# Second matmul of a PReLU feed-forward in 32-row tiles: three groups in lanes, the fourth tile fills

## The chip, the cores and the metric

The kernel runs on one core of one Trainium2 chip. The metric is the device time of one execution in microseconds (us), as the median of several runs. Engines are called as in the profile: PE is TensorE's matmuls, PEld its weight loads, DVE is VectorE, ACT is ScalarE, POOL is GpSimd, SP is SyncE, which issues DMAs here.

## The reference

Two steps follow each other: an induced set attention over four batches of 12480 tokens with 128 channels and 32 inducing points, then a feed-forward with a leaky activation and 2048 hidden features, applied to all 49920 tokens.

```
def mab(q, kv):
    a = softmax(q @ kv.T / sqrt(128))
    return a @ kv
h   = mab(inducing, x[b])      # 32 x 128, one per batch
y   = mab(x[b], h)             # 12480 x 128
z   = y @ w_in                 # 49920 x 2048
g   = max(z, 0) + alpha * min(z, 0)
out = g @ w_out                # 49920 x 128, float32
```

## The kernel before

Tokens are handled in groups of 512 (GRP), four groups to a block of 2048; a batch has six blocks and a rest of 192 tokens, so 25 groups, and there are 100 groups in all. The 2048 hidden features are 16 chunks of 128.

The attention's second step and the first matmul of the feed-forward are folded: hW = h @ w_in has only 32 rows per chunk, so the first matmul ("fill") takes the 32 rows of hW of a chunk as weights and streams the 512 unnormalized attention weights (rep) of a group. It uses 32 of TensorE's 128 rows; the four row tiles can hold four different chunks. rep holds the same 32 rows four times, once for each row tile. The activation is split as g = alpha * z + (1 - alpha) * max(z, 0): the first part is linear and goes through one small matrix per batch (hA = h @ Amat, 32 x 128), the second needs max(z, 0) alone, with (1 - alpha) scaled into w_out (W1). The softmax denominator (rd) is multiplied in at the end.

So the steps for a group are: 16 fills into PSUM banks; 16 evictions with max(., 0) to bf16 tiles gt in SBUF, on ACT (line 448) or DVE (line 450); the second matmul (mm2), in which a 128x128 block of gt (tokens) is the stationary operand and the 128x128 chunk of W1 streams, 64 matmuls per group, summed in an accumulator bank of 128x512 float32; the linear part (linear), 4 matmuls of 32 rows into the same accumulator; and the output (finish, line 503), a multiplication by rd on DVE into ob, which a DMA on POOL's queue writes out.

The work goes in slots. A slot makes four fills, one in each row tile (fill), then runs the tasks due there, then the 16 second matmuls of the slot before (mm2). A group has four slots (two for the rest of 192). PSUM's eight banks are a ring of six, given out in turn by bank(), and two accumulators, used alternately. A planner (make_plan), a beam search with fixed costs and due times, picks for each slot which of the four evictions go to ACT and where an output stands among them. Every instruction of an engine is chained to the one before it (pin), so the order on each engine is the order in which the code emits it.

Tasks are the attention's remaining steps, spread over slots by the table tasks: loading and transposing the next batch's tokens (a_load, a_xpose), its scores and sums (a_scores, a_accum), h (h_sum, h_den, h_transpose), hW and hA (h_weights, h_linear), and for each block the scores of tokens against h (b_scores), their replication by way of DRAM (b_rep) and the denominators (b_den). The first batch's h is made ahead of the first slot, on TensorE. All matmuls go through the helper mm, line 96; the tiles tell them apart in the profile.

Of the kernel before, what the change touches and what calls it, by code (L numbers as in the profile page):

```python
# [16 lines left out]
P = 128  # L17
# [4 lines left out]
RING = 6  # L22
# [3 lines left out]
def kernel(  # L26
# [47 lines left out]
    xn_pool = ctx.enter_context(tc.tile_pool(name="xnp", bufs=8))  # L74
    xt_pool = ctx.enter_context(tc.tile_pool(name="xtp", bufs=2))
    gt_pool = ctx.enter_context(tc.tile_pool(name="gtp", bufs=4))
# [9 lines left out]
    ring = [psum.tile([P, GRP], f32, name=f"ring{i}") for i in range(RING)]  # L86
    accs = [psum.tile([P, NB, C], f32, name=f"acc{i}") for i in range(2)]
    ring_n = [0]

    def bank():  # L90
        t = ring[ring_n[0] % RING]
        ring_n[0] += 1
        return t
# [59 lines left out]
    def p_xpose(st, u, i, last=False):  # L153
        xn = st.xn[u]
        if u == NS:
            tp = bank()[:].bitcast(bf16)
            for j in range(JR):
                pin(nc.tensor.transpose(
                    tp[:, j * PR : (j + 1) * PR], xn[:, j, :], ident[:PR, :PR]
                ))  # L160
            pin(nc.vector.tensor_copy(
                out=st.xTr[:].rearrange("c j p -> c (j p)"), in_=tp[:, :REM]
            ))
            return
        cut = 2 if last else 1
        for h in range(cut):
            tp = bank()[:].bitcast(bf16)
# [9 lines left out]
            if h == 0:  # L177
                pin(nc.vector.tensor_copy(out=dst, in_=tp[:, :w]))  # L178
            else:
                pin(nc.scalar.copy(out=dst, in_=tp[:, :w]))  # L180

# [8 lines left out]
    def p_scores(st, u, i):  # L190
# [9 lines left out]
        ))  # L200
        st.e1T[u, i] = e1t
# [20 lines left out]
    def warm(st, n=1):  # L222
        for _ in range(n):
            mm(
                accs[0][:, 1:, :].rearrange("p k c -> p (k c)"), ident[:],
                st.xT[:, 0, 0, : 3 * P], start=False, stop=False, skip_group_check=True,
            )
# [6 lines left out]
    def p_scale(st, et):  # L234
        ps = bank()
        mm(ps[:, 0:1], fold[:], et[:])
        st.rs = const.tile([P, 1], f32, name="rs")
        st.sc = st.rs
        pin(nc.vector.reciprocal(out=st.rs[:], in_=ps[:, 0:1]))

# [22 lines left out]
    def a_scores(st, u):  # L263
        ps = bank()
        if u < NS:
# [5 lines left out]
            ))  # L271
            e1T = work.tile([P, NB, P], bf16, name="e1T", tag="e1T")
            pin(nc.sync.dma_start_transpose(out=e1T[:], in_=e1[:]))
        else:
# [5 lines left out]
            ))  # L280
            e1T = work.tile([P, JR, M], bf16, name="e1Tr", tag="e1Tr")
# [5 lines left out]
    def a_accum(st, u):  # L287
# [3 lines left out]
        if u < NS:  # L291
# [10 lines left out]
            ))  # L302
        else:
# [7 lines left out]
            ))  # L311

# [5 lines left out]
    def h_den(st):  # L318
# [5 lines left out]
        pin(nc.vector.tensor_scalar_mul(out=st.fr[:], in0=fold[:], scalar1=rh[:]))  # L324


    def h_transpose(st):
# [3 lines left out]
        pin(nc.vector.tensor_copy(out=st.hT4[:], in_=ps[:, :P]))  # L331
        st.hT = st.hT4[:, 0:M]

    def h_weights(st, first=False):
        ps = bank()
        for r in range(4):
            mm(
                ps[32 * r : 32 * r + 32, :], st.hT,
                w_in_b[:, r * NJ * P : (r + 1) * NJ * P],
            )  # L340
        st.hW = work.tile([P, NJ, P], bf16, name="hW", tag="hW")

        for j0, j1 in ((0, 1), (1, NJ)) if first else ((0, NJ),):
            evac_h(
                st, st.hW[:, j0:j1, :].rearrange("m j k -> m (j k)"), ps[:, j0 * P : j1 * P]
            )

    def h_linear(st):
# [3 lines left out]
        evac_h(st, st.hA[:], pa[:, :C])  # L352


    def b_scores(st, s):
# [12 lines left out]

        nq = NQ if s < NS else 1
# [14 lines left out]
    def b_scores_pe(st, q):  # L384
# [6 lines left out]
        ))  # L391
        st.rep[q] = st.rep0[:, q, :]

    def b_den(st, s):
        e2 = st.e2.pop(s)
        ps = bank()
        if s < NS:
            for j in range(NB):
                mm(ps[:, j * NQ : (j + 1) * NQ], e2[:, j * P : (j + 1) * P], pick[:])
            rd = work.tile([P, NB, NQ], f32, name="rd", tag="rd")  # L400
# [3 lines left out]
        else:  # L404
            for j in range(JR):
                mm(ps[:PR, j : j + 1], e2[:, j * PR : (j + 1) * PR], pick[0:M, 0:1])
            rd = work.tile([PR, JR, 1], f32, name="rdr", tag="rdr")
            pin(nc.vector.reciprocal(
                out=rd[:].rearrange("p j q -> p (j q)"), in_=ps[:PR, :JR]
            ))  # L410
        st.rden[s] = rd
# [5 lines left out]

    held = []

    def flush():  # L420
        while held:
            finish(*held.pop())

    def fill(st, g, j):
        pp, nb, cp = shape_of(g)
        t = pp * nb
        w = t * cp
        rep = st.rep[g]
        gt = gt_pool.tile([P, 4, GRP], bf16, name="gt", tag="gt")
        banks = []  # L430
        for r in range(4):
            ps = bank()
            for i in range(cp):
                mm(
                    ps[:, i * t : (i + 1) * t],
                    st.hW[32 * r : 32 * r + 32, j * cp + i, :],
                    rep[32 * r : 32 * r + 32, :t],
                )
            banks.append(ps)
        lin = j == NJ // cp - 1 and lin_groups(st.b, g)  # L440
        if lin:
            linear(st, lin)
        bits, pos = plan[st.b * NG + g, j]
        for r, ps in enumerate(banks):
            if r == pos:
                flush()
            if bits >> r & 1:
                pin(nc.scalar.activation(out=gt[:, r, :w], in_=ps[:, :w], func=RELU))  # L448
            else:
                pin(nc.vector.tensor_relu(gt[:, r, :w], ps[:, :w]))  # L450
        flush()
        return gt

    def mm2(st, g, j, gt):
        pp, nb, cp = shape_of(g)
        acc = accs[(st.b * NG + g) % 2]
        begun = (g % 2 == 1 and st.b + g > 1) or cp > 1
        for r in range(4):
            for i in range(cp):
                c = r * NJ + j * cp + i  # L460
                for k in range(nb):
                    k0 = (i * nb + k) * pp
                    mm(
                        acc[:pp, k, :], gt[:, r, k0 : k0 + pp], W1[:, c, :],
                        start=(j == 0 and r == 0 and i == 0 and k == 0 and not begun),
                        stop=False, skip_group_check=True,
                    )
        if j == NJ // cp - 1 and st.b * NG + g > 0:
            held.append((st, g))

    def lin_groups(b, g):
        if g % 2 == 0 and (b, g) != (0, 0):
            return [g, g + 1] if g + 1 < NS * NQ else [g]
        return []

    def linear(st, groups):
        for k in range(NB):  # L480
            for r, g in enumerate(groups):
                pp, nb, cp = shape_of(g)
                if k < nb:
                    mm(
                        accs[(st.b * NG + g) % 2][:pp, k, :],
                        st.rep[g][32 * r : 32 * r + 32, k * pp : (k + 1) * pp],
                        st.hA[32 * r : 32 * r + 32, :],
                        start=((r == 1 or cp > 1) and k == 0), stop=False, skip_group_check=True,
                    )

    def finish(st, g):
        pp, nb, _ = shape_of(g)
        acc = accs[(st.b * NG + g) % 2]
# [3 lines left out]
        final = (st.b, g) == (B - 1, NG - 1)  # L497
# [8 lines left out]
        if final:  # L506
            pin(nc.scalar.activation(  # L507
                out=ob[:pp, cut, :], in_=acc[:pp, cut, :], func=COPY, scale=rd[:pp, cut, 0:1]
            ))
        t0 = st.b * N + s * SUP  # L510
# [4 lines left out]
        ending = st.b == B - 1 and g >= NG - 4  # L515
        pin((nc.sync if ending else nc.gpsimd).dma_start(out=dst, in_=ob[:pp, :nb, :]))  # L516
        st.rep.pop(g)


# [4 lines left out]
    xs = const.tile([P, NQ, GRP], f32, name="xs")  # L524
# [17 lines left out]
    w_out_f = const.tile([P, KC, C], f32, name="w_out_f")  # L542
    pin(nc.gpsimd.dma_start(out=w_in_b[:], in_=moe_w_in))
    w_out_v = moe_w_out.rearrange("(r j p) c -> p r j c", p=P, j=NJ)
# [19 lines left out]
    itp = bank()[:].bitcast(bf16)  # L564
    nc.tensor.transpose(itp[:, :M], ind_b[:], ident[:M, :M])  # L565
    nc.vector.tensor_copy(out=IT[:], in_=itp[:, :M])

# [10 lines left out]
    def alphas():  # L578
# [5 lines left out]
        ))  # L584

# [15 lines left out]
    def w_amat():  # L601
# [6 lines left out]
        pin(nc.vector.tensor_copy(out=Amat[:], in_=aps[:, :C]))  # L608

# [6 lines left out]
    pool = accs[0][:, 0, :M]  # L616
    den = accs[1][:, 0, 0:1]
# [3 lines left out]
    for i in range(n):  # L621
# [7 lines left out]
        if i == 3:  # L629
# [12 lines left out]
    h_weights(st, first=True)  # L642
# [5 lines left out]
    fills = [(b, g, j) for b in range(B) for g in range(NG)  # L648
             for j in range(NJ // shape_of(g)[2])]
    states = {0: st}  # L650
    tasks = {}


    def at(slot, fn, j=1, cost=None):
        tasks.setdefault((slot, j), []).append((fn, cost))

    def late_finish():
        linear(st, [0])
        finish(st, 0)

    at(0, lambda: warm(st, 2), 0)
    at(0, lambda: b_scores_pe(st, 1), 1, (240, "A", 480))
    at(0, lambda: b_den(st, 0), 2, (130, "D", 250))
    at(1, w_amat, 2, (950, "D", 250))
    at(1, lambda: h_linear(st), 3, (80, "D", 250))
    at(2, late_finish, 0)
    at(2, lambda: linear(st, [1]), 0)

    for b in range(B):
        base = b * NG  # L670
        for s in range(1, NS + 1):
            g = base + s * NQ - 4
            at(g, lambda b=b, s=s: b_scores(states[b], s), 3, (320, "A", 490))
            at(g + 1, lambda b=b, s=s: b_rep(states[b], s), 3)
            at(g + 2, lambda b=b, s=s: b_den(states[b], s), 3, (130, "D", 250))
        if b + 1 < B:
            n = b + 1

            def begin(n=n):
                states[n] = new_batch(n)  # L680

            at(base, begin)
            for i, u in enumerate(order):
# [131 lines left out]
```

## Time and profile before

| | |
|---|---|
| Time, median of 3 runs (lowest, highest) | 592.75 us (592.55, 592.86) |
| Profiled execution: span from first to last instruction | 591.0 us |
| Time outside the span, against the median | 1.75 us |
| PE, PEld, DVE, ACT, POOL busy | 578.7, 434.2, 517.7, 502.5, 84.9 us |
| First fill, end of the last second matmul | 25.5, 587.7 us |
| Granted TensorE clock | 1.000 |
| DMA | 70.10 MB, mean 119 GB/s |

All times are us from the start of the span unless marked ns. A line of a group gives line, engine, operation, output<-input, partitions x elements, and a count; then the busy time, the mean ns of one, the idle time of the engine just before them, and what ended most of that. "32*128" ahead of a matmul's shape says that it uses 32 rows and 128 columns of the array. A matmul's duration reaches from its start to its modelled end; matmuls overlap, so the distance of their starts is what a stream of them costs. In a timeline, a line is start, length, engine, operation and how many were merged into it.

### The profile page before, as it was taken

How to read it: one execution, taken by the hardware profiler on the slowest of the kernel's cores; microseconds unless marked ns; L12 is line 12 of the kernel's file. 1: busy time of each engine (PE TensorE's matmuls, PEld its weight loads, DVE VectorE, ACT ScalarE, POOL GpSimd, SP SyncE). 2: the span in 40 equal slices, each digit the busy share in tenths (PEclk: the TensorE clock that was granted, in tenths of full speed). 3: DMA queues.
4: the chain of work that ended last, by engine and by line, in shares of the span. 5: the costliest groups of instructions: out<-in, count | busy, mean ns of one | idle time of the engine just before them, and what ended most of it. 6: DMA issues, size and time to landing. Idle time of an engine off the chain costs nothing.

```text
span 591.0 us, 21769 instructions
## 1 busy us (share of the span) xinstructions
PE 578.7 (98%) x9218; PEld 434.2 (73%) x9219; DVE 517.7 (88%) x869; ACT 502.5 (85%) x988; POOL 84.9 (14%) x170
## 2 busy tenths in 40 slices
PE   5999999999999999999999999999999999999997
PEld 4677777777777777777777777777777777777776
DVE  3688998999889989998989899988988998998996
ACT  2579888888889988888888998888888988989987
POOL 6631111101011111110111111101101101101100
PEclk9999999999999999999999999999999999999999
DMA  9973978751237569953126597985122221221211
GB/s 198 210 174 90 177 149 163 154 140 55 86 87 165 125 128 185 171 137 92 60 83 142 121 163 129 185 159 131 59 70 80 89 93 54 92 91 56 94 47 62
DMA packets 81825, 70.10 MB, mean 119 GB/s; under 512 B 55440, under 2 KB 71072, under 8 KB 81728
## 3 DMA queue, kind: packets, MB, share of 16 engines
q0 software_dynamic: 12528, 38.51, 26.0%
q1 hardware_dynamic: 69056, 29.68, 25.0%
q8 instruction: 72, 1.18, 0.8%
q10 hardware_dynamic: 144, 0.52, 0.2%
q14 instruction: 25, 0.20, 0.1%
HBM read 40.20 MB, written 28.75 MB: 117 GB/s over the span
## 4 chain that ended last, share of the span: by engine, by line
PE 97%; DVE 1%; DMA 1%; ACT 1%; issue 0%; SPq 0%
PE acc L96 68%; PE ring L96 27%; PE ring L172 1%; DMA ind_f<-in_inducing_dram 1%; ACT gt L448 0%; DVE xT L178 0%; DVE gt L450 0%; DVE ob L503 0%; DVE xn L612 0%; ACT xT L180 0%; SPq L526 0%; ACT ob L507 0%; DVE hT L246 0%; DVE ind_b L562 0%; PE ring L565 0%
## 5 line engine op out<-in xcount | busy, mean ns | idle before, releaser
L448 ACT ACTIVATE gt<-ring 128x512 bf16<-128x512 f32 x899 | 469.5, 599 | 67.8 <-ACT gt L448 27.4
L450 DVE TENSOR_SCALAR gt<-ring 128x512 bf16<-128x512 f32 x669 | 435.1, 685 | 52.2 <-PE ring L96 37.8
L96 PE MATMUL acc<-W,gt 128*128 128x128 bf16 x6272 | 417.9, 220 | 0.2 <-DVE ob L503 0.2
L96 PEld LDWEIGHTS <-gt 128*128 128x128 bf16 x6272 | 352.4, 98 | 79.6 <-issue 76.8
L96 PE MATMUL ring<-rep,hW 32*128 32x512 bf16 (+1 forms) x1600 | 157.3, 379 | 0.0
L516 POOL DMA_DIRECT2D out_dram<-ob x96 | 51.8, 540 | 476.5 <-DVE ob L503 412.6
L96 PEld LDWEIGHTS <-hW 32*128 32x128 bf16 x1600 | 41.1, 91 | 41.6 <-issue 0.5
L503 DVE TENSOR_TENSOR ob<-acc,rd 128x512 f32<-128x512 f32 x96 | 65.4, 681 | 2.5 <-PE acc L96 2.5
L96 PE MATMUL acc<-hA,rep 32*128 32x128 bf16 x392 | 19.8, 214 | 0.0
L96 PEld LDWEIGHTS <-rep 32*128 32x128 bf16 x392 | 15.6, 93 | 5.6
L129 POOL DMA_DIRECT2D xn<-in_x_dram x28 | 15.3, 551 | 3.3 <-DMA xn<-in_x_dram 2.4
L197 ACT ACTIVATE e1t<-ring 128x256 bf16<-128x256 f32 (+1 forms) x13 | 4.8, 371 | 10.5 <-PE ring L96 10.4
L178 DVE COPY xT<-ring 128x1024 bf16<-128x1024 bf16 (+1 forms) x12 | 8.0, 669 | 5.2 <-PE ring L172 4.8
L361 ACT ACTIVATE e<-ring 128x512 bf16<-128x512 f32 x18 | 11.0, 612 | 0.0
L269 ACT ACTIVATE e<-ring 128x512 bf16<-128x512 f32 x18 | 10.9, 605 | 0.0
L96 PE MATMUL ring<-xT,hT 128*32 128x512 bf16 (+1 forms) x97 | 10.0, 389 | 0.0
L172 PE MATMUL ring<-ident,xn 128*128 128x128 bf16 x96 | 8.8, 249 | 0.9 <-DVE xn L612 0.9
L172 PEld LDWEIGHTS <-xn 128*128 128x128 bf16 x96 | 6.8, 112 | 1.0 <-DVE xn L612 1.0
L96 PEld LDWEIGHTS <-hT 128*32 128x32 bf16 (+1 forms) x122 | 3.7, 92 | 5.1 <-issue 2.6
L96 PE MATMUL ring<-xn,e1T 128*32 128x128 bf16 x288 | 7.4, 221 | 0.0
L96 PE MATMUL ring<-xT,IT 128*32 128x512 bf16 x72 | 7.2, 390 | 0.0
L565 PE MATMUL ring<-ident,ind_b 32*128 32x32 bf16 x1 | 0.2, 205 | 6.1 <-DVE ind_b L562 6.1
(87 smaller groups left out, 113.6 us busy)
## 6 DMA issues: line engine op xcount, KB each, us to landing
out_dram<-ob POOLq DMA_DIRECT2D x93, 256.0 KB, 2.9
rep<-e2d SPq DMA_DIRECT2D x92, 128.0 KB, 3.4
xn<-in_x_dram POOLq DMA_DIRECT2D x18, 512.0 KB, 6.7
e2d<-e SPq DMA_DIRECT2D x24, 128.0 KB, 2.0
xn<-in_x_dram POOLq DMA_DIRECT2D x10, 256.0 KB, 8.5
w_out_f<-in_moe_w_out_dram POOLq DMA_DIRECT2D x4, 256.0 KB, 11.1
out_dram<-ob SPq DMA_DIRECT2D x3, 256.0 KB, 2.3
xs<-in_x_dram ACTq DMA_DIRECT2D x1, 512.0 KB, 4.9
```

Of the source, the lines that this page charges most:

```text
L96: return pin(nc.tensor.matmul(o, lhsT, rhs, start=start, stop=stop, **kw))
L129: pin(nc.gpsimd.dma_start(out=xn[:, i * w : (i + 1) * w, :], in_=src[:, i * w : (i + 1) * w, :]))
L172: pin(nc.tensor.transpose(tp[:, k * P : (k + 1) * P], xn[:, q, j * C : (j + 1) * C], ident[:]))
L178: pin(nc.vector.tensor_copy(out=dst, in_=tp[:, :w]))
L197: pin(nc.scalar.activation(out=e1t[:pp, :nb, :].rearrange("p k m -> p (k m)"), in_=ps[:pp, : nb * M], func=EXP, scale=scale,))
L269: pin(nc.scalar.activation(out=e1[:], in_=ps[:], func=EXP, scale=scale, accum_out=st.es[:, u : u + 1]))
L361: pin(nc.scalar.activation(out=e2[:], in_=ps[:], func=EXP, scale=scale_of(st)))
L448: pin(nc.scalar.activation(out=gt[:, r, :w], in_=ps[:, :w], func=RELU))
L450: pin(nc.vector.tensor_relu(gt[:, r, :w], ps[:, :w]))
L503: pin(nc.vector.tensor_tensor(out=ob[:pp, :cut, :], in0=acc[:pp, :cut, :], in1=rbc, op=MULT))
L516: pin((nc.sync if ending else nc.gpsimd).dma_start(out=dst, in_=ob[:pp, :nb, :]))
L565: nc.tensor.transpose(itp[:, :M], ind_b[:], ident[:M, :M])
```

## The change

The second matmul is split by rows for 13 of the 16 chunks (NROW). A chunk's 128x128 matmul becomes four matmuls of 32 rows each, one per row tile. Three groups are worked on at a time, each in a lane; a lane stays in one row tile for a stretch and moves to the next tile for the next, so that after four stretches a group has had all four quarters of its 13 chunks. Lanes start one stretch apart, with one stretch in four without a start. A round of a stretch takes the next chunk of each lane: four steps (k) of up to three pieces, each with its own 32x128 block of gt as weights and 32 rows of W1 streaming, and one fill in the fourth row tile. The first round of a lane in a stretch also has one of the four linear matmuls. A lane's chunk is left out of a round where its eviction is not done yet by the code's own clock, and the fill where no bank is due to be free.

After the stretch stands a drain of TensorE; then come outputs, the other three chunks of the groups as whole 128-row matmuls (whole), and the tasks of that cycle. There are 126 such cycles. The first two groups, the four rests of 192 tokens and two of the last groups do not go in lanes: the first two are done in eight opening slots as before, the others with whole chunks between stretches.

The ring and the two accumulators become one pool of eight banks: bank() takes the idle bank that is free soonest, and drained() returns it, with times from a running clock (clk), which also decides between ACT and DVE for each eviction in place of make_plan. gt tiles hold one chunk, 64 of them instead of 4 of four chunks. hW is kept for all 16 chunks in each of the four row tiles (h_weights: four matmuls and four evictions instead of four small matmuls side by side and one eviction). To make room, xs and w_out_f share a buffer and there are six xn buffers instead of eight.

```diff
+NBANK = 8
+NROW = 13
+AHEAD = 2
+KEPT = 60
...
-    xn_pool = ctx.enter_context(tc.tile_pool(name="xnp", bufs=8))
+    xn_pool = ctx.enter_context(tc.tile_pool(name="xnp", bufs=6))
-    gt_pool = ctx.enter_context(tc.tile_pool(name="gtp", bufs=4))
+    gt_pool = ctx.enter_context(tc.tile_pool(name="gtp", bufs=KEPT + 4))
...
     def bank():
-        t = ring[ring_n[0] % RING]
-        ring_n[0] += 1
-        return t
+        i = min(idle, key=lambda i: clk.free[i])
+        idle.remove(i)
+        clk.pe = max(clk.pe, clk.free[i])
+        return banks[i]
+
+    def drained(t, engine, ns, pe=0, after=190):
+        clk.pe += pe
+        start = clk.pe + after
+        if engine == "A":
+            clk.act = end = max(clk.act, start) + ns
+        else:
+            clk.dve = end = max(clk.dve, start) + ns
+        i = number[id(t)]
+        clk.free[i] = end + 170
+        idle.append(i)
...
+    def h_weights(st):
+        st.hW = hw_pool.tile([P, KC, P], bf16, name="hW", tag="hW")
+        for j in range(NJ):
+            ps = bank()
+            mm(ps[:], st.hT4[:], w_in_b[:, j * GRP : (j + 1) * GRP])
+            dst = st.hW[:, j * NJ : (j + 1) * NJ, :].rearrange("m j k -> m (j k)")
+            if st.rs is None and j % 2:
+                pin(nc.scalar.copy(out=dst, in_=ps[:]))
+                drained(ps, "A", 490, 220)
+            else:
+                evac_h(st, dst, ps[:])
+                drained(ps, "D", 620, 220)
...
+    def fill(ch, f):
+        b, g, u = ch
...
+        ps = bank()
+        for i in range(cp):
+            mm(
+                ps[:, i * t : (i + 1) * t],
+                st.hW[32 * f : 32 * f + 32, u * cp + i, :],
+                st.rep[g][32 * f : 32 * f + 32, :t],
+            )
+        gt = gt_pool.tile([P, GRP], bf16, name="gt", tag="gt")
+        after = 206 + w * 0.42
+        ca, cd = 52 + w * 0.83, 74 + w * 1.04
+        ready = clk.pe + after
+        if max(clk.act, ready) + ca <= max(clk.dve, ready) + cd:
+            pin(nc.scalar.activation(out=gt[:, :w], in_=ps[:, :w], func=RELU))
+            drained(ps, "A", ca, after=after)
+        else:
+            pin(nc.vector.tensor_relu(gt[:, :w], ps[:, :w]))
+            drained(ps, "D", cd, after=after)
+        seen[ch] = gt, clk.free[number[id(ps)]]
+
+    def piece(ch, k, rows=slice(0, P)):
+        b, g, u = ch
+        pp, nb, cp = shape_of(g)
+        i, n = divmod(k, nb)
+        return add(
+            b, g, n, seen[ch][0][rows, k * pp : (k + 1) * pp],
+            W1[rows, u * cp + i, :],
+        )
+
+    def whole(ch):
+        clk.pe = max(clk.pe, seen[ch][1])
+        for k in range(4):
+            piece(ch, k)
+        clk.pe += 226
+        spent(ch[0], ch[1], 4)
+        seen.pop(ch)
...
+        for c in range(cycles + 1):
+            t = SESSIONS + 1 + c
+            work = [
+                ((y[0], y[1]), [(*y, u) for u in range(NROW)], (c + lane_of[y]) % 4)
+                for y in laned if first[y] <= c < first[y] + 4
+            ]
+            f = (c + 3) % 4
+            ahead = c + AHEAD
+            while True:
+                run, busy = [], any(w for _, w, _ in work)
+                for y, w, q in work:
+                    if w and w[0] in seen and seen[w[0]][1] <= clk.pe + 100:
+                        if len(w) == NROW:
+                            linear(*y, q, c - first[y])
+                        run.append((w.pop(0), q))
+                opening = None
+                soon = need and need[0][0][0] <= ahead and len(seen) < KEPT
+                room = min((clk.free[i] for i in idle), default=1e9)
+                must = need and need[0][0][0] <= c
+                short = any(w for _, w, _ in work)
+                if not short and opens[c + 1] and not must:
+                    opening = opens[c + 1].pop(0)
+                elif not (soon and (must or room <= clk.pe + 60)):
+                    soon = False
+                if not (run or busy or opening or must):
+                    break
+                for k in range(4):
+                    for ch, q in run:
+                        piece(ch, k, slice(32 * q, 32 * q + 32))
+                    if k == 0 and soon and not opening:
+                        fill(need.pop(0)[1], f)
+                if opening:
+                    linear(*opening, f)
+                clk.pe += 226
...
+            clk.pe += 100
+            pin(nc.tensor.drain())
+            flush()
+            for ch in wholes[c]:
+                whole(ch)
+            flush()
+            run_tasks(t)
+            clk.pe += 100
```

## Prediction

> **What bounds the kernel now.** I read the page first: busy times, then the chain that ended last, then the groups of instructions.
>
> ```profile
> PE 578.7 (98%) x9218; PEld 434.2 (73%) x9219; DVE 517.7 (88%) x869; ACT 502.5 (85%) x988; POOL 84.9 (14%) x170
> ...
> PE 97%; DVE 1%; DMA 1%; ACT 1%; issue 0%; SPq 0%
> ...
> L448 ACT ACTIVATE gt<-ring 128x512 bf16<-128x512 f32 x899 | 469.5, 599 | 67.8 <-ACT gt L448 27.4
> L450 DVE TENSOR_SCALAR gt<-ring 128x512 bf16<-128x512 f32 x669 | 435.1, 685 | 52.2 <-PE ring L96 37.8
> L96 PE MATMUL acc<-W,gt 128*128 128x128 bf16 x6272 | 417.9, 220 | 0.2 <-DVE ob L503 0.2
> ...
> L96 PE MATMUL ring<-rep,hW 32*128 32x512 bf16 (+1 forms) x1600 | 157.3, 379 | 0.0
> ```
>
> TensorE carries 97% of the chain and its matmuls wait for nobody (the idle column is 0.0 to 0.2 us). But the page warns that a busy PE need not be at its peak, so the next view is the timeline of PE over two and a half slots of the main loop.
>
> ```profile
> 199.90 1.07 PE L96 MATMUL acc<-W,gt 128*128 128x128 bf16 x16
> 200.90 0.40 PE L96 MATMUL ring<-rep,hW 32*128 32x512 bf16 x4
> 201.23 1.07 PE L96 MATMUL acc<-W,gt 128*128 128x128 bf16 x16
> 202.23 0.40 PE L96 MATMUL ring<-rep,hW 32*128 32x512 bf16 x4
> ```
>
> A slot (4 fills, 16 second matmuls) lasts 202.23 - 200.90 = 1.33 us; the single starts in the trace give 1.327 in 280 of 392 slots. Inside, second matmuls start 55.6 ns apart, and the four fills, in four row tiles, start 3 ns apart; one fill streams 216 ns (a linear matmul in a fill's own tile starts 216 ns behind it). Streaming is thus 16 x 55.6 + 216 = 1.106 us. The other 0.22 us is change of form: the last second matmul to the first fill takes 152 ns instead of 56 (0.10 lost), the last fill to the next second matmul 317 instead of 216 (0.10 lost), and 10 ns go to the four starts. So about 0.2 us x 392 = 78 us of the span is TensorE changing between full-array and 32-row form. That is what the change can attack.
>
> **Can three lanes and a fill share the array?** Two places of the timeline bear on it.
>
> ```profile
> 37.78 0.61 PE L96 MATMUL ring<-rep,hW 32*128 32x512 bf16 x4
> 38.01 0.61 PE L96 MATMUL acc<-hA,rep 32*128 32x128 bf16 x8
> ...
> 111.78 0.41 PE L96 MATMUL ring<-xn,e1T 128*32 128x128 bf16 x16
> ```
>
> At 38.01 a linear matmul in one row tile starts 4 ns behind a 512-column fill in another and seven more follow 56 ns apart while that fill still streams: short and long ones do not hold each other up. Where the linear runs in pairs (206.43), two row tiles step together, 4 ns apart, every 55.6 ns, each with its own weights. At 111.78 sixteen weight-and-matmul pairs in four column tiles take four steps of 55.5 ns: 13.9 ns a pair. A round of the change has 12 pieces and one fill in four steps, 222.4 ns, which is 17.1 ns a pair. No row shows three row tiles with new weights in every step over a long stretch. Bounds: 222 ns (the tiles as independent as in these rows) and 325 ns (13 pairs at the 25 ns at which single-tile matmuls with four columns, ring<-pick,e, follow each other). I take 222: the rows with concurrent tiles are the nearest.
>
> The Trainium skill speaks against this. "TensorE: Matmul & The Clock Gate", Part 3, gives four row tiles of K=32, N=512 a measured speedup of 3.07, not 4. By that a round would be 222.4 x 4 / 3.07 = 290 ns, and the sum below would be 112 us longer, a clear loss. Here the fills, just that case, start within 10 ns and the next in the tile follows at 216 ns, which is nearer 3.8; the page's figure may hold the start and end of a single quartet.
>
> **The sum**, from the instruction order of the changed program (built, not run) and rows of the trace. Of 100 groups, 92 run in lanes.
> - To the first fill: 25.5 us now. The first hW eviction is 128x512 (680 ns for that form) instead of 128x128 (351): 25.8.
> - Eight opening slots as today, 8 x 1.327, and a closing piece of four fills, two whole chunks and linears, 0.9. DVE's four hW evictions, 0.61 start to start, take 2.4 instead of 0.88 for two: beyond the 0.3 above it is 1.2 late for its fills, and PE meets full banks. (W1's last quarter, done on POOL at 23.94 + 4.06 = 28.0, is needed in the second slot already; that falls into the same 1.2.) 12.7.
> - 125 stretches hold 1665 rounds (107 stretches have the planned 13; the others more, where a lane's chunk is not yet evicted). 1665 x 0.2224 = 370.3.
> - Linear: each lane's first round has a fifth step in its tile: 125 x 0.0556 = 7.0.
> - Whole chunks between the stretches: 342 x 4 x 0.0556 = 76.1.
> - Change of form, into whole chunks and out again, 0.10 each: 125 x 0.20 = 25 (now 78).
> - The drain ahead of the whole chunks: no row shows it in the loop. Below: 0, since the change of form empties the array anyway (its 152 ns). Above: a matmul lasts 219 ns from start to end and a sequencer's wait 51, so 270 instead of 152 is 0.12. I take 0.08: 10. Behind it on PE stand the whole chunks; who waits for those is DVE's output of a group that ends there, with evictions queued behind it.
> - Tasks (scores, denominators, sums, h): the 392 slots run 41.3 us over 1.327; 50 linear passes of 0.23 are 11.3 of it; 30 remain. h_weights as four full matmuls (4 x 0.216) instead of four side by side adds 0.65 x 3: 32.
> - Waits for a bank. Below: 0. Above: a stretch offers 13 fills in 2.95 us, the engines take one per 0.267 us (ACT 0.477 and DVE 0.608 start to start); with all banks full at its start 13 need 3.47, 0.52 too much, 65 us in all. But 133 of the rounds have no fill just where no bank comes free, and see the balance below: 8, near the lower end; 25 as a fair upper one.
> - Tail behind the last matmul, 591.0 - 587.7: 3.3.
>
> 25.8 + 12.7 + 370.3 + 7.0 + 76.1 + 25 + 10 + 32 + 8 + 3.3 = 570.2 us of span, against 591.0. The profiled execution's span is 1.75 us below the median of 592.75, so the forecast is **572 us** (-3.5%). With drains and waits at nothing: 554. With drains at 0.12 and waits at 25: 594.
>
> **What is late next.** Evicting. ACT and DVE starts cost, in the main part, 1585 full evictions (192-column ones in proportion), 96 outputs of 0.608 and small ones: DVE 74 us and ACT 26 us beside the evictions, and 477a + 26000 = 608d + 74000 with a + d = 1585 balances at 471 us each; nine more hW evictions make it 473. Now they have 562 us, then 541: 87% on both. They are covered as long as gt buffers (64 tiles, about two cycles ahead) let them work in front of the lanes.
>
> **Off the path.** The DMA queues: the counts on POOL and SP stay (157 and 193 rows in both). w_out_f now shares a buffer with xs, so its DMA waits for the two copies of xs, with the constants of POOL behind it; but it was issued at 12.2 us, when both copies are done. Out-DMAs and loads share POOL's queue as before; loads are issued some 12 us before their transpose (6.7 us to landing), rep three cycles (12 us) before its first fill (3.4 us). If that cover were gone, PE would wait some us at each of 24 reps.
>
> **Rivals.**
> 1. *The stream of instructions does not keep up (slower).* Place: TensorE's own stream. PE has 47122 instructions instead of 18418, and a round needs 26 in 222 ns. For it: the instruction queue
>
> ```profile
> q8 instruction: 72, 1.18, 0.8%
> ```
>
> brings 16 KB a packet (18418 instructions of 64 B are 1.18 MB, so 256 in each), now one per 8.2 us; a packet takes 0.8% x 16 x 591 / 72 = 1.05 us. In a stretch one is needed each 2.2 us, some 180 over the loop. Small DMAs of this trace need 2.0 to 3.4 us from issue to landing (e2d<-e, rep<-e2d). Fetched one by one at 3.4, 180 take 612 and the kernel 25.8 + 612 + 3.3 + 1.75 = 643 us. It decides from (592.75 - 30.9) / 180 = 3.1 us a fetch on; equally from a round of 235 ns on, since (592.75 - 572) / 1665 = 12.5 ns. Against it: fetches can overlap, and at 429.0 in the trace 33 PE instructions follow a semaphore wait at 8.5 ns each, the pace needed, though only over 0.28 us.
> 2. *The evicting engines become the bound.* Fills stop between stretches: 2.7 whole chunks (0.60), forms and drain (0.28), tasks (0.25), about 1.1 us in 125 places. With three accumulators out of eight banks, at most five banks are queued, 1.3 us of work, and the next fill needs 0.42 us to its eviction (25.47 to 25.89). With five full banks the engines idle 0.2 us each time, with half as many 0.87. At 0.65, nearer the upper end, 473 + 125 x 0.65 = 554, and with 25.8, 3.3 and 1.75 the time is 585; at 0.87 it is 613, and it is a loss from 0.71 on. Against it: fills run up to two cycles ahead, and PE's 541 leaves room for 0.54 us of idleness per stretch.
> 3. *Better:* drains hidden and no bank waits: 554.
> That nothing changes form less is excluded by the instruction order: whole chunks fall from 1568 to 372.
>
> **Chances.** Forecast (560 to 585) 0.55; better (below 560) 0.09; engines (585 and more) 0.13, of which 0.08 faster, 0.02 within 0.2%, 0.03 slower; instruction stream or tiles in each other's way (over 594) 0.23. Faster by over 0.2% (which is about what a measurement of this kernel can tell from no change): 0.55 + 0.09 + 0.08 = 0.72; same 0.02; slower 0.03 + 0.23 = 0.26. The range for 8 in 10 leaves out a few in 100 below 553 and the far part of rival 1: 553 to 612.
>
> **What would show it.** Right: piece starts 55.6 ns apart in each tile, 222 ns rounds, stretches of about 3.0 us, cycles of 4.2 us; mean idle of ACT and DVE halved; PE's fill groups waiting little. Rival 1: equal gaps between matmuls with no releaser ("issue") inside stretches, at every 256th instruction or everywhere. Rival 2: PE ended by ACT or DVE at fills, and both engines over 92%. Wrong altogether: a drain that costs over 0.3 us, a step of three tiles at 75 ns or more, or outputs held up behind DVE.

## The result, and the profile after

| | before | after |
|---|---|---|
| Time, median (lowest, highest) | 592.66 us (592.55, 592.86) | **812.36 us** (805.19, 824.12) |
| Ratio of the faster executions, 95% interval | | **1.366** (1.359 to 1.374) |
| Profiled execution: span | 591.0 us | 822.4 us |
| PE instructions (matmuls and weight loads; the page counts some 20 more in each) | 18418 | 47122 |
| Instruction fetches (q8) | 72 | 184 |
| Granted TensorE clock, mean | 1.000 | 0.931 |

The kernel is slower by 37%, where 572 us (553 to 612) was forecast. The ratio leaves out the slowest execution of after, 824.12 us, which is the profiled one (granted clock 0.931, in the other three 0.939 to 0.956), and what follows uses its own span. From the page of after (busy times, clock by slice, instruction queue, chain by engine, groups of instructions):

```profile
PE 628.4 (76%) x23571; PEld 537.3 (65%) x23571; DVE 511.5 (62%) x852; ACT 521.6 (63%) x1016; POOL 84.9 (10%) x170
...
PEclk9999988898999898989999998889999999999999
...
q8 instruction: 184, 3.01, 1.5%
...
PE 73%; issue 22%; DMA 2%; ACT 1%; DVE 1%; DVEq 0%; ACTq 0%; POOLq 0%
...
L122 PE MATMUL bank<-W,gt 32*128 32x128 bf16 (+1 forms) x20624 | 568.2, 223 | 164.3 <-issue 153.4
...
L508 ACT ACTIVATE gt<-bank 128x512 bf16<-128x512 f32 (+1 forms) x921 | 483.3, 603 | 232.6 <-PE bank L122 230.8
L511 DVE TENSOR_SCALAR gt<-bank 128x512 bf16<-128x512 f32 (+1 forms) x647 | 418.9, 684 | 229.3 <-PE bank L122 225.0
L122 PE MATMUL bank<-rep,hW 32*128 32x512 bf16 (+1 forms) x1600 | 437.0, 395 | 10.9 <-issue 8.7
```

PE fell from 98% busy to 76%. The evicting engines did not take its place: ACT and DVE are at 63% and 62% and idle 230.8 and 225.0 us for PE. What PE waits for is "issue", which means that the profile shows no semaphore and no engine that released it: 22% of the chain. The waits view of after gives the same (engine, what waited, releaser: total us, times, longest us):

```profile
PEld L122 <- issue: 248.2, 342, 9.2
...
PE bank L122 <- issue: 167.2, 154, 9.0
```

The timeline of PE shows what such a wait looks like inside a stretch (start, length, merged instructions, idle time before in brackets):

```profile
300.60 0.37 PE L122 MATMUL bank<-rep,hW 32*128 32x512 bf16 x1
...
300.81 0.37 PE L122 MATMUL bank<-rep,hW 32*128 32x512 bf16 x1
...
301.03 0.37 PE L122 MATMUL bank<-rep,hW 32*128 32x512 bf16 x1
...
301.24 0.37 PE L122 MATMUL bank<-rep,hW 32*128 32x512 bf16 x1
301.26 0.50 PE L122 MATMUL bank<-W,gt 32*128 32x128 bf16 x17
305.38 0.21 PE L122 MATMUL bank<-W,gt 32*128 32x128 bf16 x1 [3.62 <-issue]
305.39 0.39 PE L122 MATMUL bank<-rep,hW 32*128 32x512 bf16 x1
...
305.61 0.54 PE L122 MATMUL bank<-rep,hW 32*128 32x512 bf16 x1
305.62 0.72 PE L122 MATMUL bank<-W,gt 32*128 32x128 bf16 x15
306.04 0.60 PE L122 MATMUL bank<-rep,hW 32*128 32x512 bf16 x1
```

The fill of each round marks its start: 300.60, 300.81, 301.03, 301.24, so rounds last 0.21 to 0.22 us. This is the forecast's round, with its three lanes stepping every 55.6 ns in the raw starts. Then PE stands still for 3.6 us and resumes slowly: from 305.61 to 306.04 a round takes 0.43 us, and the raw starts show steps of 107 ns. Counted through all of PE's records, its waits and drains included, the pauses around this place come after records 16065, 16321, 16577 and 16833, exactly 256 apart, which is one fetched block. Of the 103 pauses of over 0.8 us in the whole trace 98 stand at such a place. The fetch packet before PE resumed here ended at 303.98, 1.4 us earlier; over the 98 pauses the median is also 1.40 us.

The clock adds to it. Its record in after is 1.0 or 0.5 and nothing between, with 113.9 us at 0.5, from 305.7 to 309.1 among them, where rounds take 0.43 us. None of the 60 pauses of 0.8 to 1.5 us is followed by half clock, 10 of the 28 of 1.5 to 2.5 us are, and 11 of the 12 longer ones.

### The profile page after: what moved, and what is told of

The parts are those of the page before. It is cut to its first block, busy times and chain, and to the rows that moved or that the text cites. A ratio compares the mean times of both kernels' runs of the same rounds, so it can differ in the third digit from the quotient of the medians.

```text
span 822.4 us, 50064 instructions
## 1 busy us (share of the span) xinstructions
PE 628.4 (76%) x23571; PEld 537.3 (65%) x23571; DVE 511.5 (62%) x852; ACT 521.6 (63%) x1016; POOL 84.9 (10%) x170
## 4 chain that ended last, share of the span: by engine, by line
PE 73%; issue 22%; DMA 2%; ACT 1%; DVE 1%; DVEq 0%; ACTq 0%; POOLq 0%
PE bank L122 73%; DMA xn<-in_x_dram 2%; ACT gt L508 1%; DVE gt L511 0%; PE bank L201 0%; DVE hW L288 0%; DVE hacc L335 0%; ACT e L302 0%; ACT xT L210 0%; DVE ob L557 0%; ACT ob L561 0%; DVE hT L279 0%; DVE hA L288 0%; DVE et L353 0%; DVEq L557 0%
## 5 line engine op out<-in xcount | busy, mean ns | idle before, releaser
L122 PE MATMUL bank<-W,gt 32*128 32x128 bf16 (+1 forms) x20624 | 568.2, 223 | 164.3 <-issue 153.4
L122 PEld LDWEIGHTS <-gt 32*128 32x128 bf16 (+1 forms) x20624 | 499.6, 98 | 222.0 <-issue 217.1
L508 ACT ACTIVATE gt<-bank 128x512 bf16<-128x512 f32 (+1 forms) x921 | 483.3, 603 | 232.6 <-PE bank L122 230.8
L511 DVE TENSOR_SCALAR gt<-bank 128x512 bf16<-128x512 f32 (+1 forms) x647 | 418.9, 684 | 229.3 <-PE bank L122 225.0
L122 PE MATMUL bank<-rep,hW 32*128 32x512 bf16 (+1 forms) x1600 | 437.0, 395 | 10.9 <-issue 8.7
L122 PEld LDWEIGHTS <-hW 32*128 32x128 bf16 x1600 | 142.5, 92 | 11.6 <-issue 10.0
L557 DVE TENSOR_TENSOR ob<-bank,rd 128x512 f32<-128x512 f32 x96 | 65.4, 682 | 12.7 <-PE bank L122 12.6
L122 PE MATMUL bank<-hA,rep 32*128 32x128 bf16 x392 | 32.8, 229 | 0.7 <-DVE hA L288 0.4
L400 ACT ACTIVATE e<-bank 128x512 bf16<-128x512 f32 x18 | 10.8, 600 | 18.1 <-PE bank L122 18.1
L302 ACT ACTIVATE e<-bank 128x512 bf16<-128x512 f32 x18 | 10.8, 601 | 15.7 <-PE bank L122 15.7
L122 PE MATMUL bank<-xT,hT 128*32 128x512 bf16 (+1 forms) x98 | 11.0, 398 | 0.1
```

The source lines that it names most:

```text
L122: return pin(nc.tensor.matmul(o, lhsT, rhs, start=start, stop=stop, **kw))
L302: pin(nc.scalar.activation(out=e1[:], in_=ps[:], func=EXP, scale=scale, accum_out=st.es[:, u : u + 1]))
L400: pin(nc.scalar.activation(out=e2[:], in_=ps[:], func=EXP, scale=scale_of(st)))
L508: pin(nc.scalar.activation(out=gt[:, :w], in_=ps[:, :w], func=RELU))
L511: pin(nc.vector.tensor_relu(gt[:, :w], ps[:, :w]))
L557: pin(nc.vector.tensor_tensor(out=ob[:pp, :cut, :], in0=acc[:pp, :cut, :], in1=rbc, op=MULT))
```

## Experiments

Theory I: the fetch of TensorE's instructions sets the pace; blocks of 256 come some 3.5 us apart, and a stretch needs one per 2.2 us. Rival T: narrow matmuls in three or four row tiles, each with new weights, hold each other up in the array or in the weight loads. Under I the number of instructions decides, under T their form.

**The streams alone** (e4_stream). The kernel's work is left out; it runs five streams of weight loads and matmuls with no semaphore inside them. A stream is given by its rounds, the rows of a tile and the columns streamed; 64 DMAs of 256 KB each, on SP's and POOL's queues, run beside the last.

```
+    stream("one", 768, 128, 128)
+    stream("two", 640, 64, 128)
+    stream("four", 512, 32, 128)
+    stream("wide", 256, 32, GRP)
...
+    for i in range(64):
...
+        (nc.sync, nc.gpsimd)[i % 2].dma_start(out=dst, in_=load[:])
+    stream("busy", 512, 32, 128)
```

> No kernel, but TensorE streams alone, one after the other: 768 full-array matmuls of 128 columns, 1280 in two 64-row tiles, 2048 in four 32-row tiles, 1024 in four 32-row tiles with 512 columns, and again 2048 of 128 columns in four tiles while 64 DMAs of 256 KB write to HBM. Nothing is evicted in between. Theory I: 55.6 ns a matmul for the first, 27.8 for two tiles, then not 13.9 but about 26 ns for four tiles (3.3 us for 128 pairs), 54 ns for 512 columns, and over 28 ns with the DMAs; gaps at every 256th instruction. Theory T: 13.9 ns in both streams of four tiles if the tiles are independent, more at an even pace if they are not.

Busy time in the five streams, by windows (PE, PEld, DVE, POOL with counts, then granted clock, DMA share, GB/s):

```profile
6.40:52.00 45.60, 45.60 (x767) 45.60 (x768) 0.00 (x0) 0.00 (x0) 1.00 0.01 2
52.20:88.70 36.50, 36.50 (x1281) 36.42 (x1280) 0.69 (x1) 0.00 (x0) 1.00 0.04 12
88.90:145.50 56.60, 33.70 (x2045) 31.04 (x2048) 1.29 (x2) 0.00 (x0) 0.97 0.04 14
146.50:205.00 58.50, 58.50 (x1023) 37.65 (x1024) 1.74 (x3) 0.00 (x0) 0.97 0.06 20
206.00:284.20 78.20, 43.78 (x2048) 41.21 (x2047) 1.70 (x3) 17.28 (x32) 0.80 0.64 231
```

The time per matmul is the window by the count. Full array: 45.6 / 768 = 59 ns (55.6 once warm). Two tiles: 36.5 / 1280 = 28.5, half of that as it should be. Four tiles of 128 columns: 56.6 / 2048 = 27.6, no better than two, though PE is busy for only 33.7 of the 56.6 us. With DMAs running it is 38.2. The timeline of the third stream shows how the time is lost:

```profile
101.70 1.97 PE L57 MATMUL four<-w 32*128 32x128 bf16 x128 [1.49 <-issue]
105.70 1.97 PE L57 MATMUL four<-w 32*128 32x128 bf16 x128 [2.04 <-issue]
109.16 1.05 PE L57 MATMUL four<-w 32*128 32x128 bf16 x61 [1.49 <-issue]
```

128 matmuls, which with their weight loads are 256 instructions, run at 1.75 us / 128 = 13.7 ns from start to start, which is four tiles at full pace; then PE waits 1.5 to 2.0 us for the next 256. The fetches come 3.36 to 3.97 us apart, about 3.48 in the middle. That is 3.48 / 256 = 13.6 ns per instruction. Rival T is refuted for the burst: four tiles with new weights each do run at four times one tile's pace, for as long as there are instructions. While the 64 DMAs run, fetches are 7.0 to 7.6 us apart, and afterwards 3.5 again.

**W1 stationary** (e1_w_stationary). The same stretches, lanes, fills and tiles, but a 32x128 block of W1 is the weights and a group's 512 tokens stream, so that one matmul takes the place of four; the sum then stands with features in the partitions, so a group's output is left transposed.

```
     def piece(ch, k, rows=slice(0, P)):
         ...
+        if cp == 1:
+            if k == 0:
+                add(b, g, None, W1[rows, u, :], seen[ch][0][rows, :])
+            return
```

> Same lanes, rounds, fills, evictions, drains and whole chunks, but W1 is stationary and the 512 tokens of a chunk stream in one matmul instead of four of 128: the same 216 to 222 ns per tile and round with 16378 PE instructions instead of 47122 (the output is left transposed within a group, its denominators misapplied). Theory I (TensorE's instructions arrive too slowly: 256 at a time, no closer than 3.3 us): a round now needs 8 instructions in 222 ns, one piece of 256 lasts over 7 us, the stalls with no releaser go, the clock stays at 1.0, time 570 to 600 us. Theory T (three lanes and a fill, the drains or the banks are slow by themselves): nothing of this is changed, time stays above 750 us.

Measured: 613.55 us (612.42 to 616.62), ratio 1.037 (1.034 to 1.040), 16378 PE instructions, 64 fetches a median of 9.1 us apart. Busy times and two groups from its page:

```profile
PE 571.5 (94%) x8199; PEld 269.6 (44%) x8199; DVE 499.3 (82%) x852; ACT 505.1 (83%) x1016; POOL 85.2 (14%) x170
...
L122 PE MATMUL bank<-gt,W 32*128 32x512 bf16 (+1 forms) x5124 | 493.5, 378 | 14.0 <-issue 1.1
...
L122 PE MATMUL bank<-rep,hW 32*128 32x512 bf16 (+1 forms) x1600 | 412.2, 371 | 3.8 <-DMA rep<-e2d 2.4
```

The array streams the same columns in the same tiles, and 199 us are gone; idle time by "issue" is 1.1 us in place of 153.4. From the first start of a stretch to its last, the 125 stretches add up to 381.1 us against 587.8 in after. Of these 207 us, 177.9 are pauses of over 0.2 us in after's stretches that stand at a block's end. So four 32-row tiles at work together come near what the forecast took, and it was the number of instructions that did not go through. This run has a quarter of the lanes' weight loads too, so by itself it does not exclude that these hold each other up; the bursts of e4 (13.7 ns for a matmul with new weights) and the rounds of 0.21 to 0.22 us in after do. The 613.55 is above the 600 that theory I allowed; the table under "Why the prediction was wrong" says where that went.

**A half and three quarters of the pieces** (e2_two_steps, e3_three_steps). Only the first two, or three, of a round's four steps have pieces, so part of the second matmul is left out; the fills and everything else stay.

```
-                    for ch, q in run:
+                    for ch, q in run if k < 2 else ():     # k < 3 in e3
```

> Only two of the four steps of a lane's round are issued (half of the lanes' products is left out); the fill still takes 216 ns a round, so the round's length by the array is unchanged. 27986 PE instructions, 14 a round, 15.9 ns for each. Theory I: slower than the 12.8 ns at which instructions can arrive (3.27 us for 256, the closest two fetches in the changed kernel), so hardly a stall: 570 to 620 us. Theory T, if it is drains, forms or banks: above 750; if it is the array shared by lanes: somewhere between.

> Three of the four steps (a quarter of the lanes' products is left out). 37554 PE instructions, 20 a round, 11.1 ns for each. Theory I: 147 fetches at the 3.9 us that is the median in the changed kernel make 573, at its mean of 4.3 us 632, plus the start of 30: 610 to 680 us, between the two neighbours and nearer to neither by the array's work. Theory T (drains, forms, banks): as with two steps and with four, above 750.

Measured: 645.21 us with 27986 PE instructions and 110 fetches, and 696.49 us with 37554 and 147 (one run each). Both lie above their ranges, by 25 and 16 us. The fill in the fourth tile takes the whole round either way, so the array's time is the same in e2, e3 and after. One line of the waits view of each, e2, e3:

```profile
PE bank L122 <- issue: 27.6, 90, 7.2
```

```profile
PE bank L122 <- issue: 80.9, 145, 4.0
```

27.6, 80.9 and 167.2 us of waiting rise with the instructions alone. Taking away the pieces of one step leaves some 32.5 thousand instructions, or 127 blocks, in e3's stretches, which last 460.6 us: 3.63 us a block. In after they hold some 42.1 thousand, 165 blocks in 587.8 us: 3.57. In e2 the 23 thousand, or 90 blocks, take 399.9 us, 4.4 us a block: not limited on average, and still 19 us over e1. So something is lost below the mean pace too, for which both ranges had allowed too little. The clock shows where: 108 stretches of e2 ran wholly at full clock and took 2.97 us each, no more than e1's 123 at full clock (3.02). The other 17, with 58.2 us at half clock, took 4.65 us each. In after 98 stretches at full clock took 4.21 us each, 27 with half clock 6.47; there the long pauses lie in the same stretches, so that half clock and pauses are not told apart. At full clock too after is 1.2 us a stretch above e1. Why e2 falls to half clock as often as it does was not taken apart.

**Instructions added to the kernel before** (e6_fills_in_four, e7_both_cut). In the first a 512-column fill becomes four of 128 columns in the same tile; in the second the second matmuls are cut in two halves of 64 columns as well. The streamed columns, tiles and slots stay. The lines are shown for full groups, simplified.

```
+        for c0 in cuts:                     # 0, 128, 256, 384
+            for r in range(4):
+                mm(banks[r][:, c0 : c0 + P], st.hW[32 * r : 32 * r + 32, j, :],
+                   rep[32 * r : 32 * r + 32, c0 : c0 + P])
...
+        for n0 in (0, C // 2):              # e7 only
+            mm(acc[:pp, k, n0 : n0 + C // 2], gt[:, r, k0 : k0 + pp],
+               W1[:, c, n0 : n0 + C // 2], ...)
```

> The kernel before, with each 512-column fill issued as four of 128 columns, tile after tile, so that the array streams the same: 27634 PE instructions instead of 18418, 56 a slot of 1.33 us, 23.7 ns for each. Theory I: instructions can arrive every 13.7 ns with quiet queues and every 28 with full ones, so no change where the queues are quiet and stalls at some fetches: 593 to 610 us. If instructions as such cost TensorE time (each its own issue): 9216 more at 3 ns or more, evenly in every slot.

> The kernel before, with fills in four and also each second matmul as two of 64 columns: 40178 PE instructions, 96 a slot. By the array a 64-column matmul takes 29 ns instead of 27.8, so a slot is 1.37 us and the kernel 608; an instruction is needed every 14.3 ns. Theory I: that is the pace of the fetch with quiet queues and faster than with full ones: 157 fetches at 3.9 to 4.4 us (median and mean in the changed kernel) make 612 to 690, plus some 30 of start: 640 to 700 us, with PE stalls that no releaser ends. Without theory I: 600 to 615 us.

Measured: e6 602.38 us, ratio 1.017 (1.014 to 1.020), with 27634 PE instructions and 108 fetches; e7 701.62 us, ratio 1.182 (1.178 to 1.186), with 40178 and 157, just above the top of theory I's range. The timeline of PE in e7:

```profile
302.03 0.40 PE L96 MATMUL ring<-rep,hW 32*128 32x128 bf16 x16
302.37 0.58 PE L96 MATMUL acc<-W,gt 128*128 128x64 bf16 x14
305.07 0.70 PE L96 MATMUL acc<-W,gt 128*128 128x64 bf16 x18 [2.13 <-issue]
305.70 0.40 PE L96 MATMUL ring<-rep,hW 32*128 32x128 bf16 x16
```

Here the old kernel, with no lanes and no change of plan, has the same wait in the middle of a run of full-array matmuls. Sixteen narrow fills in four tiles take 302.37 - 302.03 = 0.34 us, as four wide ones did (0.33), so the cut itself costs the array nothing. e7's slot has 96 instructions in 1.33 us, 13.8 ns each, right at the pace of e4; e6's has 64 (32 matmuls with their weight loads, not the 56 expected), 20.7 ns each, and loses 10 us. The rival on record for e6, 3 ns or more for each of the 9216 added instructions, would have been 28 us or more. In e7, 68 pauses of over 0.25 us at a block's end make 73.1 us of the 109 lost. The limit is thus a pace, not a number of tiles.

**Output DMAs left out** (e5_no_output_dma). after without its output DMAs, but for the last ones.

```
-        pin((nc.sync if ending else nc.gpsimd).dma_start(out=dst, in_=ob[:pp, :nb, :]))
+        if ending:
+            pin(nc.sync.dma_start(out=dst, in_=ob[:pp, :nb, :]))
```

> The changed kernel without the output DMAs of all but the last groups (some 92 of 100 outputs are left unwritten): 24 MB less on the DMA queues, all else as it was. Theory I with its second part (a fetch also waits behind other transfers: 3.5 us in the streams with quiet queues, 7.2 with 64 DMAs under way): the fetches come closer, the time falls by 30 to 80 us. Theory I without that part, or theory T: within 10 us of the changed kernel's 805 to 824.

Measured: 789.93 us (one run), 22 below after's median and 15 below its fastest run; less than the 30 to 80 expected. Fetches are a median of 3.88 us apart against 3.95, a mean of 4.16 against 4.35. So most of the loss is there without these DMAs; that they slow the fetches by a little fits the one run, but one run does not show it.

**The drain alone** (e8_before_drain). The kernel before, with a drain between the fills of a slot and its second matmuls.

```
+            pin(nc.tensor.drain())
             mm2(*prev)
```

> The kernel before with a drain of TensorE between the fills and the second matmuls of every slot, 391 in all: the price of a drain where the form changes anyway. The prediction's 0.08 us each gives +31 us; the 0.18 us read from the changed kernel (0.33 us from the last piece to the first whole chunk, against 0.15 from form to form without a drain) gives +70 us if nothing hides it.

Measured: 688.77 us, span 687.0 against 591.0. The timeline of PE:

```profile
300.89 0.40 PE L96 MATMUL ring<-rep,hW 32*128 32x512 bf16 x4
301.49 1.06 PE L96 MATMUL acc<-W,gt 128*128 128x128 bf16 x16 [0.20 <-issue]
302.49 0.40 PE L96 MATMUL ring<-rep,hW 32*128 32x512 bf16 x4
```

From the last fill to the next second matmul it is 583 ns in the raw starts, where it was 317: +0.266 us. Times 391 slots this is 104 us, and the span grew by 96 (some of the drains may stand where PE waited anyway). Both prices put on record for it, 0.08 and 0.18, were too low for this place.

No version tried beats the kernel before. At 3.48 us a block, e4's pace, the 184 blocks of after would need 640 us whatever the order, and 600 even at 3.26, the closest two fetches of any run, and W1 stationary, which has the fewest instructions, is at 613.55 before its outputs are turned back.

## Why the prediction was wrong

**The step that failed: "I take 222".** The term of 1665 rounds x 0.2224 = 370.3, with 7.0 for the linear part, was to be 377.3; with their last step the stretches took 587.8 + 125 x 0.056 = 595. The bounds on record (222 and 325 ns) were of the array's and the sequencer's making; the round measured, 595 / 1665 = 357 ns, lies outside both, since neither row was limited by fetching. What stands in its place is 165 blocks x 3.57 us = 588, fetch pauses and half clock together.

**Its price was known and was given too little weight.** Rival 1 is what happened: gaps with no releaser, at every 256th instruction, as "what would show it" had described them, though not equal (a median of 1.4 us, ten of them over 3.5). The half clock that follows the long ones was in no rival. Its threshold, 3.1 us a fetch, was right in kind, and so was its guess of 3.4 (e4: 3.48). Two arguments were set against it, and both fell. "Fetches can overlap": in no run here do they start closer than 3.26 us, while a packet lasts 1.04 us. "33 PE instructions at 8.5 ns each": these were instructions already there, as the 128 matmuls and their weight loads are that run at full pace after a pause in e4; a burst shorter than a block says nothing of the supply. The kernel before could not have shown the limit, since its fetches lay 4.35 to 10.75 us apart; that is a reason for an open bound, not for the lower end.

**Its size was too small as well:** 643 against 812. It took the fetches as the whole loop's pace, 180 x 3.4. But a block's wait is hardly made up later: between stretches PE uses few instructions and is slow for other reasons, and that this saves up little for the next stretch is argued from the table, not tested. By the places of the span, against the forecast of 570.2:

| | forecast | after | e1 |
|---|---|---|---|
| up to the first stretch (25.8 + 12.7) | 38.5 | 40.6 | 40.2 |
| stretches, last step included (370.3 + 7.0, bank waits 8) | 385.3 | 594.8 | 408.1 |
| between stretches (76.1 + 25 + 10 + 32) | 143.1 | 179.2 | 154.5 |
| behind the last stretch (3.3) | 3.3 | 7.8 | 7.9 |
| span | 570.2 | 822.4 | 610.7 |

(A last step is 0.056 us in after and 0.216 in e1, times 125, counted to the stretches and off what lies between.) The stretches hold 209.5 of the 252 us by which the span was missed, and what lies between 36. Of the latter, e1, with nearly the same code there, has 11; the other 25 go with after's half clock (29.1 us of this time) and its pauses at a block's end (22.0 us), which no run separates.

**Tiles.** That lanes and fill do not hold each other up was right: 0.21 to 0.22 us a round where instructions are there, and e1's stretches 6% above the forecast (408.1 against 385.3; what the 22.8 us are is not separated). The Trainium skill's page "TensorE: Matmul & The Clock Gate", Part 3, was weighed with its factor of 3.07 for four row tiles. The stream of 512-column matmuls in four tiles took 58.5 us / 1024 = 57.1 ns each, where one tile would need 216: a factor of 3.78. So the measurement decides for the tiles and against that figure here; the loss it would have foretold came, but not from there.

**Drains.** 10 us on record (0.08 each, at most 0.12). From the last piece to the next instruction it is 0.33 us in the median, where change of form alone took 0.15: 0.18 x 125 = 22 us. Behind fills it is 0.266 (e8). The bound of 0.12 took the sequencer's wait at 51 ns; what a drain adds beyond that was never in a row.

**Engines, banks, wholes.** Rival 2 is refuted: ACT and DVE are idle for over a third of the span, behind PE. Waits for a bank, 8 us on record, are hardly to be seen: PE's idle time put down to ACT or DVE in the stretches of e1 is below 1 us. Waits shorter than the 0.16 us by which a 512-column record (0.37 us) outlasts its streaming (0.216) would not show there, so they may be part of e1's 22.8 us. Change of form, whole chunks and tasks cannot be far off, since e1 spends 154.5 there against 143.1 with the drain's excess in it.

**Chances.** The forecast's own case had 0.55, all that ends slower 0.26. A stretch needed a block per 2.2 us, and no row had shown two fetches closer than 4.35; with so little known of the supply, rival 1 deserved more than a part of 0.23.

## What to carry to other kernels

Count the instructions of TensorE's stream stage by stage, weight loads included, and set them against the rate at which blocks of 256 arrive: here 3.5 us with quiet queues (13.6 ns an instruction), about 4 in this kernel, 7 and more with the queues full of e4's DMAs. A change that cuts the same streaming into more and narrower matmuls saves array time only as long as it stays above that; e6 at 20.7 ns an instruction lost 1.7%, e7 at 13.8 lost 18%. A short burst in the trace shows what the sequencer can pass on, never what the fetch can supply, so where a change raises the count severalfold, look at the instruction queue's packets first. Then look at the clock's record: here the long pauses also brought half clock, and with it rounds of 0.43 us in place of 0.22.

## What the runs showed of the hardware

- TensorE's instructions come in blocks of 256 (after: 184 packets of 16 KB for 47122), and in none of these runs did two fetches start closer than 3.26 us, though a packet takes 1.04 us; after a pause PE resumes a median of 1.40 us behind the packet's end (8 in 10 of after's 98: 1.26 to 1.53). What fills the rest of the interval is not shown.
- The Trainium skill's "Runtime: NRT & Kernel Launch", section "Instruction fetch mechanics", has the next block fetched while the current one executes and calls the crossing mostly hidden. The 256 agree; hidden it is only where a block lasts longer than the fetch: in e4 each crossing of the third stream cost about 1.7 us.
- DMAs slow the fetch: 7.0 to 7.6 us with 64 large ones in flight (e4, 231 GB/s), in after a median of 4.9 us where other packets fill over 80% of the 16 DMA engines' time between two fetches (24 cases) against 3.9. In the stall shown above the engines were at 0.97 from 298 to 301, mostly with packets of POOL's queue, and the fetch began at 302.81.
- After a long pause TensorE mostly runs at half clock for a while: 11 of the 12 pauses over 2.5 us in after, none of the 60 from 0.8 to 1.5 us; steps are then 107 ns in place of 55.6. The mean granted clock was 0.931 in after and 0.80 in e4's last stream.
- A drain of TensorE cost 0.18 us behind 128-column matmuls (after) and 0.266 behind 512-column ones (e8), beyond the change of form.
